# The small loads of a decode kernel in fewer pieces: 32 rows of w4 in one load, the last rows of wo in three loads instead of eight

## The chip, the cores and the metric

The kernel runs on one core of a Trainium2 chip. A core has a matrix engine (PE, with its own stream of weight loads, PEld), a vector engine (DVE), a scalar engine (ACT), a general engine (POOL) and a queue engine (SP) that here does nothing but issue loads and the one store. Sixteen DMA engines move the data from memory. The metric is the device time of one launch in microseconds (us); less is better. All tensors are bfloat16 in memory.

## The reference

One decode step for one token of width 512. The token is normalised; from it come an attention branch over the last 4096 positions of a cache with 32 heads of 128, and a gated MLP branch. The result is `x + attention * silu(mlp)`.

```python
x = A_x                                   # [1, 1, 512]
xn = _layernorm(x, axis=-1)
# attention: 32 heads of 128, the last W = 4096 of 32768 cached positions
q = (xn @ wq).reshape(1, 1, 32, 128).transpose(0, 2, 1, 3)
k, v = k_cache[:, :, Sk - W:, :], v_cache[:, :, Sk - W:, :]
p = softmax(einsum("bhqd,bhkd->bhqk", q, k) * 128 ** -0.5)
s = einsum("bhqk,bhkd->bhqd", p, v).transpose(0, 2, 1, 3).reshape(1, 1, 4096) @ wo   # wo [4096, 512]
# MLP: with one token the shifted parts are zero, so hs = zeros @ w2
x1 = xn + hs
h2 = gelu(_layernorm(x1) @ w3) @ w4       # w3 [512, 1376], w4 [1376, 512]
g = silu(x1 + h2)
return x + s * g
```

Keys and values of the window are 32 MB each; `wq` and `wo` are 4 MB each. In all the profile counts 78.84 MB that are read from memory.

## The kernel before, in words

Everything is loaded through one helper, `load` (L78, L79), which issues on SP's queue and keeps the order in which the program is written. All of these issues therefore carry line 79 in the profile. Two tiny loads of the token go through ACT's queue.

The weights of the MLP come first: `w2`, `w3`, `w4`. The 1376 rows of `w4` are kept in three parts. 1024 rows fill `w4_sb[:, 0:8, :]`, 8 rows on each of the 128 partitions. The last 32 rows, of 1 KB each, stand in the ninth slot, `w4_sb[0:32, 8, :]`; they are fetched by two loads, one of 7 rows and one of 25. The 320 rows in between go to `w4_few`, by two loads of 20 partitions with 8 KB each. (The profile's names leave digits out: `w_sb` is w2, w3 or w4, and `w_few` is `w4_few`.) Then `wq` follows with 4 MB.

The 32 heads are worked on in 8 groups of four, in a loop over `s` from 0 to 9 with an instruction order on PE, DVE and ACT that is written out by hand. In turn `s` the keys of group `s` (4 MB, `load_kv`) are loaded, and the values of group `h = s - 2`. A group's scores are made half on DVE (multiply, L330, and reduce, L332) and half on PE (transposes, L346, copies by ACT, L348, and matmuls, L354). A softmax follows. The values of groups 0 to 6 are multiplied by `v_part` in wide matmuls (L429), those of group 7 in narrow ones (L438). There are three buffers for keys and two for values, so a load waits until its buffer has been read.

The output projection takes `wo` in blocks of heads: 0 to 15, 16 to 23 and 24 to 27 by `load_wo`, and the last four heads by row. For these, `wo_rows` holds 128 rows of 1 KB for each of the heads 28 to 31. In the last turns the values of group 7 are loaded in four pieces (`cuts`: columns 0 to 64, 64 to 96, 96 to 112 and 112 to 128), so that PE can begin on the first of them. Behind them come the loads of `wo_rows`: for each of the four heads one load of its first 72, 88, 104 or 120 rows, and one of the rest. So 12 loads stand on SP's queue at the end. PE then does `v_part` piece by piece, with the block of heads 24 to 27 (`y_block(2)`) between the first two; DVE divides by the softmax's sum (`v_out`, L455), and `y_head` adds the four heads by four matmuls each (`rows_add`, L157). DVE multiplies by the gate (L605) and adds the token (L607), and SP stores the row.

The tile framework gives each load one of eight completion semaphores, in turn.

Of the kernel before, what the change touches and what calls it, by code (L numbers as in the profile page):

```python
# [8 lines left out]
P = 128  # L9
# [9 lines left out]
G = 4  # L19
# [10 lines left out]
def kernel(  # L30
# [18 lines left out]
    _, H, Sk, Dh = A_k_cache.shape  # L49
# [8 lines left out]
    F = B_w3.shape[1]  # L58
# [19 lines left out]
    def load(dst, src):  # L78
        return tc.keep_in_program_order(nc.sync.dma_start(out=dst, in_=src))  # L79
# [9 lines left out]
    load(w3_sb[:], B_w3.rearrange("(p c) n -> p c n", p=P))  # L89
    w4_sb = wts.tile([P, 9, D], BF16, name="w4_sb")  # L90
    load(w4_sb[:, 0:8, :], B_w4[0:8 * P, :].rearrange("(p c) n -> p c n", p=P))
    load(w4_sb[0:7, 8, :], B_w4[F - 32:F - 25, :])
    load(w4_sb[7:32, 8, :], B_w4[F - 25:F, :])
    w4_few = wts.tile([64, 8, D], BF16, name="w4_few")
    nc.gpsimd.memset(w4_few[:], 0.0)
    for c in range(2):
# [7 lines left out]
    def load_kv(pool, cache, g, cuts=(0, CP)):  # L104
        t = pool.tile([P, CP, Dh], BF16, tag="kv", name="kv")
        src = cache[0, G * g:G * g + G, W0:, :].rearrange("a (b c) d -> b a (c d)", b=PB)
        dst = t[:].rearrange("p c d -> p (c d)")
        for c0, c1 in zip(cuts, cuts[1:]):
            load(dst[:, c0 * Dh:c1 * Dh], src[:, :, c0 * Dh:c1 * Dh])
        return t  # L110
# [43 lines left out]
    def rows_add(ps, col, w, last):  # L154
        k = col.shape[0]
        for j in range(KC):
            nc.tensor.matmul(ps[32 * j:32 * j + 1, :], lhsT=col, rhs=w[0:k, j * P:(j + 1) * P],  # L157
                             start=False, stop=last, skip_group_check=True)
# [161 lines left out]
    def k_open(g):  # L320
        st[g] = {
            "sT": ps_s.tile([P, CP - 64, G], FP32, tag="sT", name="sT"),
            "S": sm_pool.tile([P, CP], FP32, tag="S", name="S"),
        }

    def k_vector(g, kn, part):
        m = nd(g) // 4
        rows = slice(m * part, m * part + m)
        prod = prod_pool.tile([P, 20, Dh], BF16, tag="prod", name="prod")
        nc.vector.tensor_tensor(out=prod[:, 0:m, :], in0=kn[:, rows, :],  # L330
                                in1=q_bc[:, g:g + 1, :].to_broadcast([P, m, Dh]), op=ALU.mult)
        nc.vector.tensor_reduce(out=st[g]["S"][:, rows], in_=prod[:, 0:m, :], axis=AX.X, op=ALU.add)  # L332
# [3 lines left out]
    def batches(g):  # L336
        n, m = nd(g), CP - nd(g)
        k = -(-m // 8)
        edges = [n + m * i // k for i in range(k + 1)]
        return list(zip(edges, edges[1:]))  # L340

    def k_turn(g, kn, b):
        c0, c1 = batches(g)[b]
        pt = ps_tr.tile([P, 8, P], BF16, tag="pt", name="pt")
        for c in range(c0, c1):
            nc.tensor.transpose(pt[:, c - c0, :], kn[:, c, :], ident_bf[:])  # L346
        kts[b] = kt_pool.tile([P, 8, P], BF16, tag="kt", name="kt")
        nc.scalar.copy(out=kts[b][:, 0:c1 - c0, :], in_=pt[:, 0:c1 - c0, :])  # L348

    def k_scores(g, b):  # L350
        kt = kts.pop(b)
        c0, c1 = batches(g)[b]
        for c in range(c0, c1):
            nc.tensor.matmul(st[g]["sT"][:, c - nd(g), :], lhsT=kt[:, c - c0, :],  # L354
                             rhs=qT_bf[:, G * g:G * g + G], start=True, stop=True)
# [39 lines left out]
    def sm_den(g):  # L395
        s = st[g]
        s["den"] = ps_misc.tile([P, G], FP32, tag="misc", name="den_ps")
        nc.tensor.matmul(s["den"][:], lhsT=ones_f[:], rhs=s["sum"][:], start=True, stop=True)

    def sm_rden(g):  # L400
        s = st[g]
        s["rden"] = sm_pool.tile([P, G], FP32, tag="rden", name="rden")
        nc.vector.reciprocal(out=s["rden"][:], in_=s["den"][:])  # L403
# [4 lines left out]
    h_part = H - G  # L408
    o_blk, wo_blk, ox_blk = {}, {}, {}

    def load_wo(i):
        h0, n = blocks[i]
        load(wo_blk[i], A_wo[h0 * P:(h0 + n) * P, :].rearrange("(p t) n -> p t n", p=P))
# [1 line left out]
    def wo_row(h):  # L415
        return wo_rows[:, h - h_part, :]

    def load_rows(h, p0, p1):
        load(wo_rows[p0:p1, h - h_part, :], A_wo[h * P + p0:h * P + p1, :])

    def v_part(g, v, c0=0, c1=CP):
        s = st[g]
# [18 lines left out]
    def v_add(g):  # L441
        s = st[g]
        s["oT"] = ps_misc.tile([P, G], FP32, tag="misc", name="oT")
        for j in range(4):
            nc.tensor.matmul(s["oT"][:], lhsT=s["ov_sb"][:, j, :], rhs=fold[:, G * j:G * j + G],  # L445
                             start=(j == 0), stop=(j == 3))

    def v_out(g):
        h = G * g
        b = [i for i, (h0, _) in enumerate(blocks) if h >= h0][-1]  # L450
        if b not in o_blk:
            o_blk[b] = sm_pool.tile([P, blocks[b][1]], BF16, tag=f"o{b}", bufs=1, name="o")
        c = h - blocks[b][0]
        if g >= NG - 3:
            nc.vector.tensor_tensor(out=o_blk[b][:, c:c + G], in0=st[g]["oT"][:], in1=st[g]["rden"][:],  # L455
                                    op=ALU.mult)
            return
        for k in range(G):
            nc.scalar.mul(o_blk[b][:, c + k:c + k + 1], st[g]["oT"][:, k:k + 1], st[g]["rden"][:, k:k + 1])  # L459
# [51 lines left out]
    for s in range(NG + LAG):  # L511
        h = s - LAG
        last = h == NG - 1
        kn = load_kv(k_pool, A_k_cache, s, (0, 64, CP) if s == 0 else (0, CP)) if s < NG else None
        if s == LAG:
            wts_guard.__exit__(None, None, None)
            v_pool = ctx.enter_context(tc.tile_pool(name="v", bufs=V_BUFS))
            wo_blk[2] = v_pool.tile([P, 4, D], BF16, tag="wo_4", bufs=1, name="wo_4")
            wo_rows = v_pool.tile([P, H - h_part, D], BF16, tag="wo_rows", bufs=1, name="wo_rows")
        if last:  # L520
            v = load_kv(v_pool, A_v_cache, h, cuts)
            for r, p in zip(range(H - G, H), (72, 88, 104, 120)):
                load_rows(r, 0, p)
                load_rows(r, p, P)
        elif h >= 0:
            v = load_kv(v_pool, A_v_cache, h)
        if h == 3:
            wo_24 = k_pool.tile([P, 32, D], BF16, tag="kv", name="wo_24")
            wo_blk[0], wo_blk[1] = wo_24[:, 0:16, :], wo_24[:, 16:24, :]
            load_wo(0)  # L530
        if h == 5:
            load_wo(1)
            load_wo(2)

        if s < NG:
            nb = len(batches(s))

            def keys(b0, b1):
                for b in range(b0, b1):
                    k_turn(s, kn, b)  # L540
                    if b > 0:
                        k_scores(s, b - 1)

            k_open(s)
            k_vector(s, kn, 0)
            keys(0, 2)
            if s > 1:
                sm_den(s - 2)
                sm_rden(s - 2)
            if h - 1 in MOVED:  # L550
                v_add(h - 1)
                v_out(h - 1)
            if s == 7:
                rows_add(y_ps, one_f, y_row, False)
            keys(2, 4)
            k_vector(s, kn, 1)
            if s > 0:
                sm_turn(s - 1)
            if s == 6:
                ox_spread(0)  # L560
            keys(4, nb)
            k_scores(s, nb - 1)
            sm_own(s)
            if s > 0:
                sm_exp(s - 1)
            k_vector(s, kn, 2)
            if s == 6:
                ox_pick(0)
            k_vector(s, kn, 3)
            if h >= 0:  # L570
                v_part(h, v)
            sm_max(s)
            if s == 6:
                y_wide(0, 0, 16)
            if h >= 0 and h not in MOVED:
                v_out(h)
        elif s == NG:

            sm_den(NG - 2)
            sm_rden(NG - 2)  # L580
            sm_turn(NG - 1)
            sm_exp(NG - 1)
            v_add(h - 1)
            v_out(h - 1)
            ox_spread(1)
            ox_pick(1)
            sm_den(NG - 1)
            sm_rden(NG - 1)
            y_block(1)
            v_part(h, v)  # L590
            v_add(h)
            v_out(h)
            ox_spread(2)
        else:
            v_part(h, v, 0, cuts[1])
            ox_pick(2)
            y_block(2)
            for c0, c1 in zip(cuts[1:], cuts[2:]):
                v_part(h, v, c0, c1)
            v_out(h)  # L600
            for r in range(H - G, H):
                y_head(r)
# [36 lines left out]
```

## Time and profile before

| what | value |
|---|---|
| median of three runs | 196.84 us (196.53 to 197.04) |
| the profiled execution: time, span | 196.84 us, 195.0 us |
| busy: PE, DVE, ACT | 138.5 us (71%), 145.6 us (75%), 90.6 us (46%) |
| DMA: packets, bytes, mean rate | 4765, 79.08 MB, 405 GB/s |
| mean granted PE clock | 0.666 |

The span runs from the first to the last instruction; 1.84 us of the profiled execution's time lie outside it. Each "slice" of the page is a fortieth of the span, 4.9 us, and its digits are tenths of busy time. In a line of the chain the first number is the start and the second the length, both in us. A DMA's line there runs from its issue to its landing. SPq is SP's issuing queue.

### The profile page before, as it was taken

The numbers are of one execution on the slowest core, as the hardware profiler recorded it, in microseconds if no ns is written. First come the engines' busy times: TensorE is split into PE (matmuls) and PEld (weight loads), VectorE is DVE, ScalarE is ACT, GpSimd is POOL, SyncE is SP. The second block draws the span as 40 slices with busy tenths as digits, with TensorE's granted clock in tenths as the row PEclk, the third lists the DMA queues.
The fourth block names the chain that finished last, engine by engine and source line by source line (L and its number), as shares of the span: only waits on it lengthen the run. The fifth ranks groups of instructions, "written<-read, shape, count | busy, mean of one in ns | idle before, by whom it ended". The sixth has DMA issues, their size and how long they took to land.

```text
span 195.0 us, 3926 instructions
## 1 busy us (share of the span) xinstructions
PE 138.5 (71%) x1696; PEld 100.0 (51%) x1696; DVE 145.6 (75%) x168; ACT 90.6 (46%) x197; POOL 5.9 (3%) x12
## 2 busy tenths in 40 slices
PE   0548978989955169249869892974497989868852
PEld 0447248867855153248438642942483358644640
DVE  1580012999999999998999999999999988932001
ACT  2003002888778265308855752582277157861100
POOL 8210000000000000000000000000000000000000
PEclk9999985555555555855885557588555795885855
DMA  6999999999999999999999999999999999999950
GB/s 207 444 432 417 420 440 444 425 440 430 430 427 439 437 447 430 430 430 430 420 430 440 430 417 403 460 430 430 427 423 432 433 427 399 448 400 405 390 172 4
DMA packets 4765, 79.08 MB, mean 405 GB/s; under 512 B 709, under 2 KB 1253, under 8 KB 1765
## 3 DMA queue, kind: packets, MB, share of 16 engines
q1 hardware_dynamic: 4597, 78.84, 95.4%
q8 instruction: 13, 0.21, 0.4%
q10 hardware_dynamic: 152, 0.00, 0.0%
q14 instruction: 3, 0.02, 0.0%
HBM read 78.84 MB, written 0.00 MB: 404 GB/s over the span
## 4 chain that ended last, share of the span: by engine, by line
DVE 49%; PE 28%; DMA 11%; ACT 4%; issue 4%; SPq 1%; POOL 0%; POOLq 0%; ACTq 0%
DVE S L332 29%; DVE prod L330 15%; DMA kv<-in_A_v_cache_dram 8%; PE pt L346 6%; PE oT L445 4%; ACT kt L348 3%; PE hr_ps L256 3%; PE ov L429 3%; PE a_ps L237 2%; PE sT L354 2%; DMA x_bf<-in_A_x_dram 2%; PE yr_ps L493 2%; PE qT_ps L272 2%; PE hr_ps L251 1%; DVE S L368 1%
## 5 line engine op out<-in xcount | busy, mean ns | idle before, releaser
L332 DVE TENSOR_REDUCE S<-prod 128x20 f32<-128x2560 bf16 (+2 forms) x32 | 82.2, 2570 | 1.1
L348 ACT COPY kt<-pt 128x1024 bf16<-128x1024 bf16 (+1 forms) x56 | 55.2, 1006 | 16.8 <-PE pt L346 15.8
L346 PE MATMUL pt<-ident_bf,kv 128*128 128x128 bf16 x444 | 51.4, 293 | 2.4 <-DMA kv<-in_A_k_cache_dram 2.4
L346 PEld LDWEIGHTS <-kv 128*128 128x128 bf16 x444 | 41.9, 136 | 7.4 <-issue 3.5
L330 DVE TENSOR_TENSOR prod<-kv,q_bc 128x2560 bf16<-128x2560 bf16 (+2 forms) x32 | 43.5, 1359 | 1.7 <-ACT q_bc L286 1.3
L354 PE MATMUL sT<-qT_bf,kt 128*128 128x4 bf16 x444 | 20.9, 169 | 13.3 <-ACT kt L348 12.2
L354 PEld LDWEIGHTS <-kt 128*128 128x128 bf16 x444 | 17.6, 106 | 21.1 <-ACT kt L348 20.7
L429 PE MATMUL ov<-kv,pT 128*16 128x512 bf16 x224 | 22.3, 569 | 0.0
L445 PE MATMUL oT<-fold,ov_sb 128*128 128x4 f32 x56 | 11.5, 328 | 13.7 <-DVE rden L403 12.7
L445 PEld LDWEIGHTS oT<-fold,ov_sb 128*128 128x128 f32 x56 | 10.8, 289 | 14.7 <-DVE rden L403 13.2
L392 ACT ACTIVATE pT<-S,mb 128x128 bf16<-128x128 f32 x32 | 13.9, 576 | 0.3
L429 PEld LDWEIGHTS <-pT 128*16 128x16 bf16 x224 | 6.4, 116 | 12.9 <-issue 11.9
L459 ACT ACTIVATE o<-oT,rden 128x1 bf16<-128x1 f32 x20 | 3.6, 264 | 20.3 <-PE oT L445 20.3
L433 ACT COPY ov_sb<-ov 128x512 f32<-128x512 f32 x7 | 4.1, 590 | 15.3 <-PE ov L429 15.3
L455 DVE TENSOR_TENSOR o<-oT,rden 128x4 bf16<-128x4 f32 x3 | 0.5, 162 | 12.7 <-PE oT L445 8.3
L363 ACT ACTIVATE own<-sT,par 128x48 f32<-128x48 f32 (+2 forms) x32 | 7.6, 361 | 3.7 <-PE sT L354 3.7
L392 ACT ACTIVATION_READ_ACCUMULATOR pT<-S,mb 128x1 f32 x32 | 8.4, 261 | 0.0
L240 ACT ACTIVATE a_bf<-a_ps 128x8 bf16<-128x8 f32 x1 | 0.2, 178 | 14.4 <-PE a_ps L237 14.4
L259 DVE COPY hr<-hr_ps 1x512 f32<-1x512 f32 x1 | 0.7, 678 | 7.5 <-PE hr_ps L256 7.5
L376 PE MATMUL mt_ps<-ident_f,m 128*1 128x128 f32 x8 | 2.9, 360 | 4.4 <-DVE rden L403 4.4
L237 PE MATMUL a_ps<-z_bf,w_sb 128*128 128x1 bf16 (+2 forms) x68 | 4.8, 204 | 1.5 <-DVE z_bf L220 1.5
L237 PEld LDWEIGHTS <-w_sb 128*128 128x128 bf16 (+2 forms) x68 | 5.0, 166 | 1.6 <-issue 1.6
(119 smaller groups left out, 102.1 us busy)
## 6 DMA issues: line engine op xcount, KB each, us to landing
kv<-in_A_k_cache_dram SPq DMA_DIRECT2D x7, 4096.0 KB
kv<-in_A_v_cache_dram SPq DMA_DIRECT2D x7, 4096.0 KB
wq_sb<-in_A_wq_dram SPq DMA_DIRECT2D x1, 4096.0 KB
kv<-in_A_k_cache_dram SPq DMA_DIRECT2D x2, 2048.0 KB
wo<-in_A_wo_dram SPq DMA_DIRECT2D x1, 2048.0 KB
kv<-in_A_v_cache_dram SPq DMA_DIRECT2D x1, 2048.0 KB
w_sb<-in_B_w_dram SPq DMA_DIRECT2D x1, 1376.0 KB
w_sb<-in_B_w_dram SPq DMA_DIRECT2D x1, 1024.0 KB
```

What stands on the lines that cost most here:

```text
L237: nc.tensor.matmul(a_ps[0:m, j:j + 1], lhsT=w3_cols(c, j), rhs=z3_bf[:, c:c + 1], start=(c == 0), stop=(c == KC - 1))
L256: nc.tensor.matmul(hr_ps[:], lhsT=act, rhs=w, start=False, stop=(i == len(chunks) - 1))
L330: nc.vector.tensor_tensor(out=prod[:, 0:m, :], in0=kn[:, rows, :], in1=q_bc[:, g:g + 1, :].to_broadcast([P, m, Dh]), op=ALU.mult)
L332: nc.vector.tensor_reduce(out=st[g]["S"][:, rows], in_=prod[:, 0:m, :], axis=AX.X, op=ALU.add)
L346: nc.tensor.transpose(pt[:, c - c0, :], kn[:, c, :], ident_bf[:])
L348: nc.scalar.copy(out=kts[b][:, 0:c1 - c0, :], in_=pt[:, 0:c1 - c0, :])
L354: nc.tensor.matmul(st[g]["sT"][:, c - nd(g), :], lhsT=kt[:, c - c0, :], rhs=qT_bf[:, G * g:G * g + G], start=True, stop=True)
L363: nc.scalar.mul(s["own"][:, 0:m, a], s["sT"][:, 0:m, a], par[:, a:a + 1])
L392: nc.scalar.activation(out=s["pT"][:, :, a], in_=s["S"][:], func=ACT.Exp, scale=scale, bias=mb[:, a:a + 1], accum_out=s["sum"][:, a:a + 1])
L429: nc.tensor.matmul(s["ov"][r:r + 4 * G], lhsT=s["pT"][:, c:c + 4, :].rearrange("p i a -> p (i a)"), rhs=v[:, c:c + 4, :], start=False, sto ...
L433: nc.scalar.copy(out=s["ov_sb"][:], in_=s["ov"][:])
L445: nc.tensor.matmul(s["oT"][:], lhsT=s["ov_sb"][:, j, :], rhs=fold[:, G * j:G * j + G], start=(j == 0), stop=(j == 3))
```

## The change

The two loads for the last 32 rows of `w4` become one load. The eight loads for the last rows of `wo` become three: one for heads 28 and 29 together, one for head 30 and one for head 31, each over all 128 partitions. What is loaded, where it is put in the on-chip memory, and all computation stay as they were.

```diff
     load(w4_sb[:, 0:8, :], B_w4[0:8 * P, :].rearrange("(p c) n -> p c n", p=P))
-    load(w4_sb[0:7, 8, :], B_w4[F - 32:F - 25, :])
-    load(w4_sb[7:32, 8, :], B_w4[F - 25:F, :])
+    load(w4_sb[0:32, 8, :], B_w4[F - 32:F, :])
...
-    def load_rows(h, p0, p1):
-        load(wo_rows[p0:p1, h - h_part, :], A_wo[h * P + p0:h * P + p1, :])
+    def load_rows(h, n):
+        load(wo_rows[:, h - h_part:h - h_part + n, :],
+             A_wo[h * P:(h + n) * P, :].rearrange("(h p) n -> p h n", p=P))
...
             v = load_kv(v_pool, A_v_cache, h, cuts)
-            for r, p in zip(range(H - G, H), (72, 88, 104, 120)):
-                load_rows(r, 0, p)
-                load_rows(r, p, P)
+            for r, n in ((H - G, 2), (H - 2, 1), (H - 1, 1)):
+                load_rows(r, n)
```

## The prediction

> **What bounds the kernel now.** I read the slices of the page first, for what is busy when. The DMA row is full from the second slice to the 38th, while no compute engine is:
>
> ```profile
> span 195.0 us, 3926 instructions
> ...
> DMA  6999999999999999999999999999999999999950
> GB/s 207 444 432 417 420 440 444 425 440 430 430 427 439 437 447 430 430 430 430 420 430 440 430 417 403 460 430 430 427 423 432 433 427 399 448 400 405 390 172 4
> ```
>
> So the time is the loads plus what comes after the last of them. The chain that ended last, from 173 us on, says which load that is (columns: start, length, what):
>
> ```profile
> 173.67 15.92 DMA kv<-in_A_v_cache_dram
> ...
> 189.60 1.70 DMA wo_rows<-in_A_wo_dram
> ...
> 191.34 0.30 PE y_ps L157 x4
> ...
> 191.66 0.30 DVE y L605
> ...
> 191.99 0.29 DVE out_row L607
> ```
>
> The last piece of the last values lands at 189.58, and only then is the last `wo_rows` load *issued*; it lands 1.70 us later, four matmuls follow, and the store. The waits of SP's queue from 172 us on say why it was issued so late (total, times, longest):
>
> ```profile
> SPq L79 <- DMA kv<-in_A_v_cache_dram: 12.6, 5, 4.7
> ```
>
> The loads take eight completion semaphores in turn: the numbers that the trace records at their issues repeat with period eight. A load is therefore held until the one eight places before it has landed. Five of the eight `wo_rows` loads are held by values: they go out at 178.37, 183.33, 186.00, 187.39 and 189.60, each 0.01 to 0.02 us after the landing of group 6's values (178.35) and of the four pieces (183.31, 185.99, 187.37, 189.58).
>
> The third view is the trace's landing marks: each load leaves 16, one from each DMA engine that it uses and the rest at its issue. The `wq` load's come in groups: ten at 19.76 to 20.27, one at 21.54, five at 22.41 to 22.57. Those five stay behind: for group 6's values the first mark is at 174.40, the last at 178.35, and most of the final 4 us of trailing is that old. A whole 4 MB load adds 9.7 us to every engine, whether ahead or behind, and the values of the last group are issued (171.79) before the most advanced engine runs dry (174.40). So no engine ever waits, and the kernel ends when the most trailing engine has worked off its own list.
>
> Fourth, the last stretch by windows (window, its length, busy time of PE, PEld, DVE, ACT and POOL, clock, DMA share, GB/s):
>
> ```profile
> 178.00:183.50 5.50, 4.80 (x72) 2.27 (x65) 0.11 (x1) 0.59 (x1) 0.00 (x0) 0.73 0.98 410
> 184.50:186.00 1.50, 1.02 (x40) 0.93 (x41) 0.35 (x2) 0.00 (x0) 0.00 (x0) 0.50 0.86 270
> 186.00:188.60 2.60, 2.01 (x64) 1.68 (x64) 0.00 (x0) 0.00 (x0) 0.00 (x0) 0.50 0.65 199
> ```
>
> From 184.5 the engines are still 86% busy, but move a third less: while the first engines work at row pieces of 1 KB packets, a 4 KB packet of values takes 0.18 to 0.22 us instead of 0.16. This stretches the last pieces on the trailing engine. On the foremost engine the second, third and fourth piece take 2.47, 1.27 and 1.25 us; on the last one 2.68, 1.38 and 2.21, together 1.28 us more.
>
> **The profiled execution** took 196.84 us, its span 195.0 and 1.84 around it; that is also the median of the three times. All sums start there.
>
> **The w4 rows.** Two loads, of 7 and of 25 rows of 1 KB, become one of 32. The 7-row load leaves seven marks and the 25-row load five: one row on each of seven engines, then five on each of five. A load with 128 rows leaves 16; I take 16 for 32 rows as well, two rows each. A 1 KB packet took 0.046 us there, so an engine that served both pieces falls from 6 x 0.046 = 0.28 to 2 x 0.046 = 0.09: 0.18 us less. One that served neither gains 0.09. The next load, `w_few`, also leaves five marks, and moves 64 KB on each of five engines, eight packets of 8 KB at 0.31 = 2.5 us, which is just how far five engines trail afterwards. If the two fives are the same, the trailing engine gains 0.18; if not, it loses up to 0.09. I take -0.18, and keep +0.09 for the range. Since it is never idle, this reaches the end.
>
> [...]
>
> **SP's queue.** One issue fewer at the start and five fewer at the end, at 0.27 to 0.56 us each; the issues for 128 rows that remain take about 0.55 each. At the start the turns move by one place (the second half of K group 0 and K groups 1 and 2 go out behind other loads), with the engines fed until 22 us by what is already out: nothing. At the end the three row loads take turns whose holders landed by 168.63, so they go out from about 174.3 to 176, right behind the values. Behind them on SP's queue is only the output store. No wait is added on any compute engine: the merged load of heads 28 and 29 is the first of the three and its 16 rows pass before those of head 30.
>
> **The tail after the last values.** Before: 189.58 to the end of the last matmul at 191.64, 2.06 us. Afterwards two things can end last there.
>
> ```profile
> 185.94 0.59 PE L157 MATMUL y_ps<-wo,ox 128*1 128x128 bf16 x16 [0.48 <-DMA wo_rows<-in_A_wo_dram]
> ...
> 190.25 0.16 DVE L455 TENSOR_TENSOR o<-oT,rden 128x4 bf16<-128x4 f32 x1 [4.36 <-PE oT L438]
> 190.47 0.10 PEld L157 LDWEIGHTS <-o 128*1 128x1 bf16 x8 [0.34 <-DVE o L455]
> ```
>
> PE: the last values, their scaling and the start of the output rows take 190.47 - 189.58 = 0.89, and 16 such matmuls that wait for nothing 0.59 (the first line): 1.48. The rows: on the trailing engine 32 rows follow the values. In this trace the 24-row load, with which 32 rows have passed there, landed at 190.92, 1.34 after the values. Add 0.04 to release PE and 0.30 for the last four matmuls: 1.68. The larger counts: 2.06 becomes about 1.65 (three completion marks instead of six), **-0.41**. Ends: -0.58 (PE alone) and -0.05 (rows at 0.052 us each, as at 188.5 to 189: 32 x 0.052 + 0.34 = 2.0).
>
> **The stretch of the last pieces.** The change keeps 512 rows of 1 KB, but every engine now takes its 32 directly behind its values. So foremost engines are done by about 185.3 instead of coming back for more at 184.6, 187.2 and 188.65, and others take more rows than they did. The nearest rows differ: packets of 8 KB beside the 25-row load at 9.5 us were not stretched at all (0.309), those beside rows at 184.5 by a third. Ends: -1.28 (no stretch at all) and +0.4 (512 rows against the some 380 that were moved before the last values had landed, 1.28 x 132/380). I take **-0.2**: the row traffic stays, but the late pieces beside the trailing engine's last five packets (0.24 to 0.35 us each from 187.5 to 188.66) go, for about 0.3, against more rows before.
>
> [...]
>
> Sum: 196.84 - 0.18 - 0.41 - 0.20 = **196.05 us**. With the next stages (L605, L607, the store) as they were.
>
> **Rivals.**
> *The stretch goes altogether* (the pieces cause it): 196.84 - 0.18 - 0.41 - 1.28 = 195.0. For it: before 184 eleven engines read 4 KB packets at 0.16. Against: the rows remain.
> *The stretch grows*, as all rows are now out early: 196.84 - 0.18 - 0.41 + 0.4 = 196.65, no change. For it: packets of values stretched as soon as rows moved.
> *Slower: an instruction fetch on the trailing engine.* The trace has 13 fetches of 16 KB, each on one engine; the one at 33.99 put an engine that was foremost 1.54 us behind the others. Those before 187 fell on engines that were not last. The fetch order may move with the instructions left out. If one falls on the trailing engine: 196.05 + 1.54 = 197.6, or 197.8 with the stretch as before. It decides from some 1.4 us on. Against: PE's stream loses only a few waits, and the fetch at 187.21 comes when the trailing engine has only a few packets left.
> *The change does nothing*: were the row loads held by turns as before, only -0.18 is left: 196.65.
>
> **How the numbers follow.** What a measurement of this kernel can tell from no change is 0.3%, 0.59 us: 196.25 to 197.43 is "same". Forecast case 0.47, its own range 195.6 to 196.45; stretch gone 0.20; stretch grown, or nothing done, 0.23; slower 0.10. Faster: three quarters of the first and all of the second, with a little of the third, 0.60. Same: 0.31. Slower: 0.09. The range 195.1 to 196.9 leaves out a part of the second case and the slower one.
>
> **What would show it.** Right: no waits of SP's queue for values after 176; all three `wo_rows` issues before 176.5; the last four of the 16 output matmuls less than 1.7 us after the last values' landing; the 32-row load with 16 marks; five trailing engines behind by 0.2 less at `wq`. Wrong: a wait for `wo_rows` of over 0.6 us at the end; last values landing after 189.6; a landing spread of group 6's values over 4 us.

## The result, and the profile after

The changed kernel took 195.19 us (median of 6 runs, 195.06 to 195.96), the kernel before 196.98 beside it; the ratio is 0.9914 (95% interval 0.9893 to 0.9936), about 1.7 us less. In six later runs its median was 195.58 and the ratio 0.9928 (0.9901 to 0.9955). The profiled execution took 195.15 us, with 1.75 outside its span.

From the page:

```profile
span 193.4 us, 3919 instructions
...
DMA  6999999999999999999999999999999999999970
GB/s 209 426 444 417 427 427 441 425 434 430 434 430 429 434 430 434 434 434 427 424 434 434 430 434 400 458 434 434 430 427 427 425 420 392 462 420 410 396 298 5
```

The row of busy shares differs from before in the second last slice alone (7 instead of 5), and the rate of that slice is higher (298 against 172 GB/s). The chain that ended last (start, length, what):

```profile
173.74 14.60 DMA kv<-in_A_v_cache_dram
...
188.39 0.60 PE oT L440 x16
...
189.02 0.17 DVE o L457
...
189.23 0.73 PE y_ps L156 x16
```

No `wo_rows` load stands in it any more. The last values land at 188.34 (before 189.58), and the last output matmul ends at 189.96 (before 191.64). So of the 1.68 us, 1.24 were gained ahead of that landing and 0.44 behind it. The chain puts all 16 output matmuls down to PE; the trace's single records show a short wait in them. Twelve have started by 189.41, the last `wo_rows` load lands at 189.61, and the last four start at 189.66. SP's issues, and the waits of its queue from 172 us on:

```profile
171.86 2.49 SPq L79 DMA_DIRECT2D kv<-in_A_v_cache_dram  x4
174.39 1.61 SPq L79 DMA_DIRECT2D wo_rows<-in_A_wo_dram  x3
190.63 0.61 SPq L79 DMA_DIRECT2D out_dram<-out_row  x1
```

```profile
SPq L79 <- DVE out_row L608: 12.1, 1, 12.1
...
SPq L79 <- DMA kv<-in_A_v_cache_dram: 2.4, 1, 2.4
```

The row loads go out directly behind the values. One wait for values is left, from 176.0 to 178.44: what stands next in the queue then is the output store, which has nothing to store for another 12 us. By windows (length, busy PE, PEld, DVE, ACT, POOL, clock, DMA share, GB/s):

```profile
178.00:183.50 5.50, 4.80 (x71) 2.27 (x64) 0.18 (x1) 0.58 (x1) 0.00 (x0) 0.72 0.98 409
184.50:186.00 1.50, 1.08 (x41) 0.98 (x37) 0.35 (x2) 0.00 (x0) 0.00 (x0) 0.52 0.99 382
186.00:188.60 2.60, 2.18 (x72) 1.88 (x72) 0.01 (x1) 0.00 (x0) 0.00 (x0) 0.50 0.58 209
```

From 184.5 to 186 the engines move 382 GB/s at a share of 0.99, where before it was 270 at 0.86. By the landing marks, the second, third and fourth piece of the values take 2.46, 1.26 and 1.24 us on the last engine, together 4.96 instead of 6.27.

On the marks: in both traces a load of 128 partitions has 16 of them, and so has the one of 32 rows here. The smaller loads of weights have a single record at their issue and then fewer marks: 7 for the 7 rows of `w4`, 5 for the 25 and for each load of `w4_few`, and 12, 14, 11, 10, 13, 12, 15 and 8 for the `wo_rows` loads of 72, 56, 88, 40, 104, 24, 120 and 8 rows. That each mark is one engine's, with an equal share of the load, is the author's reading; no trace names the engine.

### The profile page after: what moved, and what is told of

Read it like the earlier page. It is cut to its first block, busy times and chain, and to the rows that moved or that the text cites. A ratio compares the mean times of both kernels' runs of the same rounds, so it can differ in the third digit from the quotient of the medians.

```text
span 193.4 us, 3919 instructions
## 1 busy us (share of the span) xinstructions
PE 138.4 (72%) x1696; PEld 100.3 (52%) x1696; DVE 145.6 (75%) x168; ACT 90.6 (47%) x197; POOL 5.9 (3%) x12
## 4 chain that ended last, share of the span: by engine, by line
DVE 50%; PE 29%; DMA 10%; ACT 4%; issue 4%; SPq 1%; POOL 0%; POOLq 0%; ACTq 0%
DVE S L331 29%; DVE prod L329 15%; DMA kv<-in_A_v_cache_dram 8%; PE pt L345 6%; PE oT L447 4%; ACT kt L347 3%; PE hr_ps L255 3%; PE ov L431 3%; PE a_ps L236 2%; PE sT L353 2%; DMA x_bf<-in_A_x_dram 2%; PE yr_ps L495 2%; PE qT_ps L271 2%; PE hr_ps L250 1%; DVE S L367 1%
```

## The experiments

Two explanations were to be told apart for the 1.24 us. **A**: the rows in loads of fewer than 128 partitions slow all that moves beside them, and whole loads do not. **B**: the row loads were late because their turns held them. Ratios are to the kernel before on the same chip. Unless its diff says otherwise, a kernel is the changed one. "The rows" are those of `wo_rows`.

**One part of the change alone.** Rows as changed, `w4` as before:

```diff
-    load(w4_sb[0:32, 8, :], B_w4[F - 32:F, :])
+    load(w4_sb[0:7, 8, :], B_w4[F - 32:F - 25, :])
+    load(w4_sb[7:32, 8, :], B_w4[F - 25:F, :])
```

> The change without its part on w4: the 32 rows stay in two loads of 7 and 25 rows, the last rows of wo go in three whole loads. Theory (the w4 part is worth nothing at the end, because which engine trails is set by more than those rows): the same time as the changed kernel, within 0.15 us, so about 1.7 us under the kernel before; pieces of the last values unstretched, 2.5, 1.27 and 1.27 us on the last engine. Rival (the w4 part is worth the 0.18 us that was forecast): 0.18 us slower than the changed kernel, and the last landing mark of group 6's values later by that.

Measured: 195.86 us median of 12 (195.05 to 197.13), ratio 0.9948 (0.9921 to 0.9975). The fastest run equals that of the changed kernel, but 8 of 12 lie above 195.6. In its profile (196.34 us) the pieces are as quick as in the changed kernel (2.52, 1.27, 1.26) and the last values land at 188.43. Its chain ends on PE instead:

```profile
188.52 1.81 PE oT L441 x64
...
190.57 0.62 PE y_ps L157 x12
```

PE's matmuls on the values run until 190.33, 1.9 us after they have landed, so this run says nothing against the rows' gain. It shows that PE is now close behind the DMAs; the last two experiments go into that. The expectation was missed by the median all the same: it lies 0.6 us above that of the changed kernel's 12 runs below (195.26), where 4 of 12 are above 195.6.

The other part alone, the kernel before with `w4` in one load:

```diff
-    load(w4_sb[0:7, 8, :], B_w4[F - 32:F - 25, :])
-    load(w4_sb[7:32, 8, :], B_w4[F - 25:F, :])
+    load(w4_sb[0:32, 8, :], B_w4[F - 32:F, :])
```

> Only the part on w4: one load of 32 rows, the last rows of wo in the eight pieces of before. Theory: no change that can be told, ratio 0.998 to 1.002, the last pieces stretched as before (2.7, 1.4 and 2.2 us on the last engine) and the last row load issued after the last values. Rival (w4 worth 0.18 us): ratio 0.999; both cannot be told apart by the time alone, but by the landing marks after w4_few: five engines behind the others by 0.2 us less than before.

Measured: 196.77 us (196.66 to 197.45), ratio 0.9996 (0.9986 to 1.0006). Nothing. The pieces are stretched as before (2.71, 1.42 and 2.24 us), and the end of the chain is that of before:

```profile
189.64 1.68 DMA wo_rows<-in_A_wo_dram
...
191.36 0.31 PE y_ps L156 x4
```

Alone, the part on `w4` gives nothing, and the rows alone give 1.0 us by the median (196.83 to 195.86). Whether one load for `w4` adds something beside them, or the first of these kernels had more of the long runs by chance, is not settled.

**Divided, but early.** Four loads of 72 and 56 partitions; for heads 28 to 30 together, then for 31:

```diff
-            for r, n in ((H - G, 2), (H - 2, 1), (H - 1, 1)):
-                load_rows(r, n)
+            for r, n in ((H - G, 3), (H - 1, 1)):
+                load_rows(r, n, 0, 72)
+                load_rows(r, n, 72, P)
```

> The changed kernel with the last rows in four loads of 72 and 56 rows (heads 28 to 30 together, then head 31, each 0:72 and 72:128). Four loads are too few to be held by values, so none is issued late, but their rows don't fall on the engines as a 128-partition load does. Theory A (the division of the rows stretches the values' packets): 4 KB packets at 0.18 to 0.22 us again from 184 on, the last values 0.6 to 1.3 us later than in the changed kernel, and 40 instead of 32 rows behind them on twelve engines, 0.3 us: 196.0 to 196.8 us. Theory B (what stretched them was the late issue, with rows arriving while the queues run empty): packets at 0.16, last values at 188.3, 195.2 to 195.6 us.

Measured: 196.67 us (196.41 to 197.18), ratio 0.9994 (0.9983 to 1.0005): no gain. Three of the four loads go out by 174.05, and yet:

```profile
184.50:186.00 1.50, 1.02 (x34) 0.70 (x31) 0.35 (x2) 0.00 (x0) 0.00 (x0) 0.50 0.96 252
186.00:188.60 2.60, 1.66 (x52) 1.43 (x48) 0.00 (x0) 0.00 (x0) 0.00 (x0) 0.50 0.76 216
```

The engines are 96% busy and move 252 GB/s. A 4 KB packet of values takes 0.22 us in the mean once rows move, and the last values land at 189.52. Early issue is not what the gain came from.

**Whole, but held.** Eight loads of all 128 partitions and half the columns, so that the turns hold them as before:

```diff
+            for r in range(H - G, H):
+                load_rows(r, 0, D // 2)
+                load_rows(r, D // 2, D)
```

> The changed kernel with the last rows in eight loads, each of all 128 partitions and half of the columns of one head (512-byte packets instead of 1 KB). Eight loads are held by the values as before, the last one until the last values have landed. Theory A (the division stretches, the holding delays only the tail): values unstretched, last values at 188.3; the last row load goes out then and lands 1.7 us later, tail 2.06 instead of 1.64: about 195.6 us. Theory B (the late issue stretches): last values at 189 to 189.6 and 196.3 to 197 us.

Measured: 195.81 us (195.5 to 196.8), ratio 0.9953 (0.9936 to 0.9969). The pieces run unstretched (2.51, 1.23, 1.25), and the last values land at 188.04, as in the changed kernel. What is lost is the tail:

```profile
186.81 3.15 DMA wo_rows<-in_A_wo_dram
...
190.00 0.46 PE y_ps L156 x3
```

The last matmul ends at 190.46, 2.42 us after the last values (1.62 in the changed kernel). So A is the 1.24 us, and B is only the tail.

**Even, with all engines.** Halves of 64 partitions, in loads that leave 16 marks, so four partitions to a mark, early:

```diff
+            for r, n in ((H - G, 3), (H - 1, 1)):
+                load_rows(r, n, 0, 64)
+                load_rows(r, n, 64, P)
```

> The changed kernel with the last rows in four loads of 64 rows (heads 28 to 30 together, then head 31, each 0:64 and 64:128), none issued late. [...] It parts two readings of what stretches the packets of values. By partitions (an engine that writes where other engines write): stretched again, 4 KB packets at 0.18 us and more from 184 on, last values at 189 or later, 196.2 to 196.8 us. By the number of engines (fewer than 16): unstretched at 0.16, last values at 188.3, 195.1 to 195.5 us.

Measured: 197.13 us (196.97 to 198.51), ratio 1.0019 (1.0002 to 1.0036): the worst of all. Each load leaves 16 marks, as a whole one does, but:

```profile
184.50:186.00 1.50, 1.02 (x41) 0.93 (x42) 0.35 (x2) 0.00 (x0) 0.00 (x0) 0.60 0.97 239
186.00:188.60 2.60, 1.59 (x56) 1.22 (x46) 0.00 (x0) 0.00 (x0) 0.00 (x0) 0.50 0.86 208
```

4 KB packets take 0.24 us in the mean beside the rows, and 1 KB packets 0.067 instead of 0.046. The last values land at 190.41. With the marks read as engines, uneven shares or too few engines are thereby out as the whole cause. What still differs is which partitions a load covers, or which engine writes them; no run here shows the latter.

**120 and 8 partitions.** As above with 120 in place of 64: a load of 120 partitions leaves 15 marks, so 8 partitions to a mark, as many as in a load of 128 with its 16; the 8 partitions leave eight marks.

```diff
+            for r, n in ((H - G, 3), (H - 1, 1)):
+                load_rows(r, n, 0, 120)
+                load_rows(r, n, 120, P)
```

> The rows as four early loads: partitions 0 to 120 of heads 28 to 30, partitions 120 to 128 of them, and the same two for head 31. A load of 120 partitions takes 15 DMA engines with 8 partitions each, as many for each engine as in a load of 128. Theory 1 (an engine slows the others where it writes partitions that are another engine's in the loads of values, and in those an engine has 8 neighbouring partitions): the 120-row loads are in step with the values for all but the last engine, so 4 KB packets stay at 0.16 us, the last values land at 188.2 to 188.8 and the time is 195.1 to 195.8. Theory 2 (the same, but an engine's partitions in a load of 128 are not neighbours): 4 KB packets at 0.20 to 0.33 us from 184, the last values at 189.4 to 190.4 and the time 196.5 to 197.1. Rival (any load of less than 128 partitions slows the others): as theory 2.

Measured: 196.59 us (196.24 to 197.35), ratio 0.999 (0.9968 to 1.0012). The forecast of theory 1 is missed: 4 KB packets take 0.22 to 0.26 from 186.5 to 188, and 1 KB packets 0.064 to 0.092 until 189.25. Its mechanism is not refuted by this. The first 66 rows, from 185.57 to 186.5, all belong to loads of 120 partitions; they took 0.046 us each, and the 4 KB packets beside them 0.16 from 185.75 to 186.25. The stretch sets in at 186.5, and the foremost engine, at some 0.0425 us from row to row, is through with its 24 rows at about 186.6 and comes to a load of 8 partitions. With 72 partitions the stretch came after 0.5 us of rows, well before the foremost engine had left its first load (18 rows). And two things are mixed in this profile: from 183.25 to 185.5, when no row had moved yet, the 4 KB packets were at 0.17 to 0.22 already, while those of 8 KB kept their 0.31; that is the second stretch, below. Whether the 120 partitions, the 8, or any division stretches the packets stays open.

Packets in the last stage of the profiles, in us:

| rows in loads of | 4 KB, from the first row on | 1 KB row | last values land | median time |
|---|---|---|---|---|
| before: 72 to 120 and the rest | 0.189 | 0.055 | 189.58 | 196.98 |
| 72 / 56 | 0.219 | 0.057 | 189.52 | 196.67 |
| 64 / 64 | 0.241 | 0.067 | 190.41 | 197.13 |
| 120 / 8 | 0.197 | 0.067 | 189.31 | 196.59 |
| 128, half columns | 0.161 | (0.5 KB: 0.028) | 188.04 | 195.81 |
| 128: the change | 0.162 | 0.046 | 188.34 | 195.19 |

**Is the start to be mended too?** In the changed kernel five engines trail at `wq` (five marks at 22.29 to 22.66 us, ten at 19.87 to 20.43), and the two loads of `w4_few` leave five marks each. Here there are five loads of eight partitions, every fourth one, to bring in eight engines, as the 8-row load of the kernel before has eight marks (the lines for the two old loads, the view `w4_mid` and the matching change of the mask `few` are left out):

```diff
...
+    for j in range(4):
+        load(w4_few[j:32:4], w4_mid[j:j + 1].rearrange("j e n -> e (j n)"))
+    load(w4_few[32:64:4], B_w4[8 * P + 256:8 * P + 320, :].rearrange("(e t) n -> e (t n)", e=8))
```

> The changed kernel with the 320 rows of w4_few in five loads of 8 partitions, spread over eight engines (40 KB each) instead of two loads over five engines (64 KB each). It takes 24 KB, 0.93 us, off the five engines that trail. Theory (the most trailing DMA engine sets the landing of the last values, PE's own order follows close behind): last values at about 187.4 instead of 188.34, but the output matmuls bound by PE's chain, which has some 0.4 us to give: 194.8 us. Rival (which engine trails is not set by w4_few): 195.2 us as before, last values at 188.3. Rival (DMA alone bounds the end): 194.3 us.

Measured: 196.09 us (195.69 to 197.99), ratio 0.9962 (0.9934 to 0.9989): slower than the changed kernel by 0.9, where 0.4 less was forecast. The last values land at 189.15 instead of the forecast 187.4. The spread of `wq`'s marks falls as expected, from 2.79 to 1.78 us, but all marks are late: the first is at 21.49 instead of 19.87. From 9 to 13 us, first this kernel, then the changed one:

```profile
9.00:13.00 4.00, 1.24 (x5) 1.15 (x6) 3.20 (x22) 0.00 (x0) 0.55 (x1) 1.00 1.19 401
```

```profile
9.00:13.00 4.00, 1.24 (x5) 1.16 (x6) 3.20 (x22) 0.00 (x0) 0.55 (x1) 1.00 1.09 459
```

Eight 32 KB packets of `wq` beside these loads took 2.46 to 2.94 us instead of 1.21, while the loads' own 8 KB packets kept 0.31. That this is the same stretch is not shown. And not every load of fewer than 128 partitions stretches its neighbours: in the kernels before and after, the two loads of `w4_few`, of 20 partitions and five marks, stand beside the same packets of `wq`, and from 10.5 to 13 us these took 1.21 to 1.25.

The same kernel with two of PE's blocks of output rows moved behind the values, `y_block(1)` behind `v_part` of group 6 and `y_block(2)` behind the third piece:

```diff
-            y_block(1)
             v_part(h, v)
+            y_block(1)
...
-            y_block(2)
             for c0, c1 in zip(cuts[1:], cuts[2:]):
+                if c1 == CP:
+                    y_block(2)
                 v_part(h, v, c0, c1)
```

> As the one before, and two blocks of PE's work moved: the matmuls of heads 16 to 23 behind group 6's values (into the wait for ACT's copy), those of heads 24 to 27 behind the third piece of the last values. PE gains about 1 us before the last values. Theory: now the landing of the last values bounds again: 187.4 + 1.64, 194.2 us. Rival (PE was not the bound): the same time as without the move.

Measured: 196.08 us (195.69 to 197.76), ratio 0.9963 (0.994 to 0.9985): no difference from the order here.

**PE's order.** The same move of the two blocks (the last diff) in the changed kernel, with `w4_few` as it was:

> The changed kernel with only those two blocks of PE's work moved. Theory (DMA bounds the changed kernel in most executions, PE where its clock falls earlier): median 195.1, hardly lower than the changed kernel, but with less spread upwards (195.0 to 195.4). Rival (PE bounds it): 194.7 us.

Measured: 195.05 us (194.91 to 195.8), ratio 0.9901 (0.9885 to 0.9918). Once more, with the changed kernel beside it:

> The changed kernel once more, beside the next one. Expected: a ratio of 0.990 to 0.994 to the kernel before, fastest runs at 195.0 to 195.1; the median 195.2 where PE's clock falls to half late, up to 0.7 more where it falls before the values of group 6.

> The changed kernel with the two blocks of output rows moved behind the values (y_block(1) behind v_part(6), y_block(2) behind the third piece), once more. Theory (PE's chain of values is close behind the DMAs and sets the end in the runs in which its clock falls early; the order gives it room): median 0.1 to 0.4 us under the changed kernel's and fewer runs above 195.6. Rival (the order does nothing): medians within 0.1 us.

Measured: 195.58 (194.99 to 196.14), ratio 0.9928 (0.9901 to 0.9955), and 195.05 (194.99 to 195.97), ratio 0.9912 (0.9887 to 0.9937). Over all 12 runs of each the medians are 195.26 and 195.05, with 4 and 2 runs above 195.6. The order may be worth 0.2 us; the intervals overlap.

Both profiled executions here were long ones (195.77 and 195.97), and so show what makes them. PE between 170 and 172 us in the first profile of the changed kernel, and in its second one (the third value from the right is the granted clock, 1.00 and 0.50):

```profile
170.00:172.00 2.00, 1.82 (x32) 0.62 (x31) 1.81 (x3) 1.95 (x12) 0.00 (x0) 1.00 1.04 442
```

```profile
170.00:172.00 2.00, 2.00 (x17) 0.54 (x20) 1.66 (x3) 1.95 (x11) 0.00 (x0) 0.50 1.08 459
```

In that second profile, at the clock of 0.50, the matmuls of group 5's values end at 173.43 instead of 171.85. The last values wait for their buffer, so their loads go out later:

```profile
173.48 3.00 SPq L79 DMA_DIRECT2D kv<-in_A_v_cache_dram  x4
176.52 2.00 SPq L79 DMA_DIRECT2D wo_rows<-in_A_wo_dram  x3
```

The foremost engine is done with group 6's values at 174.37 by its mark. The first 16 KB packet of the last values starts at 174.81 (173.74 in the first profile) and takes 1.31 us (0.90 there, 0.61 mostly), and the first mark of the first piece comes at 181.12 instead of 179.52. And from 183.5 to 186 the 4 KB packets take 0.20 to 0.26 us, before any row moves, while 8 KB packets stay at 0.31. The last values land at 188.94, and PE, whose clock was 0.54 from 178 to 183.5 us, is behind them too: its matmuls on them run until 189.64.

**The buffer.** As the kernel with the moved blocks, with the last values in the buffer of the keys of group 6, which is free long before:

```diff
+        if s == NG - 2:
+            k6 = kn
...
-            v = load_kv(v_pool, A_v_cache, h, cuts)
+            v = load_kv(v_pool, A_v_cache, h, cuts, k6)
```

> As the kernel with the moved blocks, but the last values go into the buffer of the keys of group 6, which is free early, instead of the one that the values of group 5 leave: their loads no longer wait for PE's multiplication of group 5's values, which ended at 171.85 in the changed kernel's profile and at 173.4 to 173.5 where PE's clock had fallen to half before it. Theory (in the later runs the loads go out after 172.9, the foremost DMA engines run dry, and the 4 KB packets of values then take 0.19 to 0.26 us with no row under way): the four issues of the last values come before 171, whatever PE's clock, 4 KB packets stay at 0.16, the last values land at 188.0 to 188.5, median 194.9 to 195.1 and at most one run above 195.6. Rival (what ends late in those runs is PE's own chain, and the DMAs don't matter): median 195.0 to 195.3, and the runs above 195.6 stay, as 2 of 12 before.

Measured: 194.96 us (194.85 to 195.03, 4 runs), ratio 0.9909 (0.9892 to 0.9925). All issues of values are done by 156.1. In the profile PE takes 3.25 us for group 5's values instead of 1.90, near the 3.07 of the long run at clock 0.50, and it costs nothing:

```profile
155.51 32.50 DMA kv<-in_A_v_cache_dram
...
188.06 0.60 PE oT L441 x16
...
188.90 0.75 PE y_ps L157 x16
```

4 KB packets are at 0.161 throughout, and the last values land at 188.01. It is the fastest kernel here. Its median is 0.3 below the changed kernel's over 12 runs, with intervals that overlap. That none of its four runs is long is what the theory says, but four are too few to prove it (at 2 in 12 none of four is long about half the time), and PE also began group 5's values 1.3 us earlier than in the long run of the changed kernel. How much of a long run is the late loads and how much PE's own chain is not settled.

## Why the prediction was right, and where not

The forecast was 196.05 us with 195.1 to 196.9 as the range; the time is 195.19. The direction is right, and the value lies at the range's lower end, since one term was taken some six times too small. What happened is the first rival: "the stretch goes altogether", at 195.0. That the time is inside the range at all, by 0.1 us, is luck: two terms were off in opposite directions, and with the 0.18 forecast for `w4` it would have been outside.

**The tail** was right, in size and in what sets it: -0.41 was said, and -0.44 measured (2.06 to 1.62). The prediction held the rows for the longer of two ways to the end (1.68 us, PE alone 1.48), and so it is: the last row load lands 1.27 us after the values (1.34 said), the last four matmuls start 0.05 later and end 0.30 after that. Without this wait they would have started at about 189.51 instead of 189.66, by the spacing of the 16 that wait for nothing. The held loads with whole partitions confirm it from the other side: there the tail is 2.42. One step on the way there was an estimate: that 32 rows had passed the trailing engine at 190.92 is rows divided by marks, added up over six loads (6 + 4 + 8 + 4 + 8 + 2). For the first four this makes 22, while the 0.83 us from 189.58 to the last mark of the 40-row load at 190.41 are 18 rows at 0.046.

**SP's queue** was right in its issues: 174.39, 175.03 and 175.55, all before 176.5. "No waits for values after 176" was not met to the letter: the store's wait until 178.44 was overlooked, and costs nothing.

**The w4 rows** were wrong: -0.18 was taken, and alone they brought nothing (ratio 0.9996; what they do beside the whole rows is open, see above). That the five engines of the 25-row load are the five of `w4_few`, on which the term rests, no run shows. The load does leave 16 marks, and the five engines do trail by less at `wq` in the mean (2.38 instead of 2.53 us behind the ten). But the last of them was at 22.66 instead of 22.57, and the spread of group 6's values was 4.20 us, above the 4 us that the prediction had named as a sign against itself. The trailing engine is one of five, picked by their scatter at `wq` (0.16 us before, 0.37 here) and by the short instruction fetches of 8 KB, which by the marks set the engine that serves them back by 0.65 to 0.95 us and hit one or two of the five; a mean over five is not the last of them.

**The stretch of the last pieces** is the step that failed. Taken was -0.2; the three pieces gave -1.31 (6.27 to 4.96), beside +0.07 at the landing of the first. Even the part that was granted was too small: in the record the trailing engine's last four packets (not five) took 0.24 to 0.35 us, together 0.48 over 0.16 each, where 0.3 was taken. The end -1.28 was in the text and was argued down: "the row traffic stays". It stays, 512 packets in both profiles, and does no harm in loads of 128 partitions: 0.162 us for a 4 KB packet beside rows at 0.046. In the kernel before, all 31 packets of 4 KB that start from 184.6 to 185.1 took 0.18 to 0.22 us. That they stretched alike is no sign against the pieces as the cause: with 72/56 and 64/64 too, every 4 KB packet that starts from 184.5 to 185 takes 0.23 us or more, and the 64/64 halves, which by their 16 marks share the work most evenly, suffer most (0.241 us in the mean).

That the division causes the stretch is shown, by the runs with whole and divided loads: 4 KB packets take 0.161 and 0.162 us beside rows in whole loads, 0.219 and 0.241 beside 72/56 and 64/64, and from 184.5 to 186 us the engines move 382 GB/s beside the change's whole loads, 252 and 239 beside these. By what mechanism it does is not shown; the run with 120 and 8 partitions (0.22 to 0.26 us from 186.5 to 188) does not settle it, and which engine writes which partitions no run here shows.

**The slower rival**, a fetch on the trailing engine, did not occur in the profile: the fetches of 16 KB cost an engine some 1.55 us each again by the marks, but none hit the trailing one.

## What to carry to other kernels

Where loads move beside a stream of 128-partition loads, try them at 128 partitions first: the same bytes in pieces of 64 to 120 partitions and their rests made the 4 KB packets beside them 17 to 49% longer at the end of this kernel (0.189 to 0.241 us instead of 0.162), and loads of eight strided partitions stood beside doubled packets at its start (2.46 to 2.94 us instead of 1.21). It is no law: two loads of 20 partitions cost the packets of `wq` nothing (1.21 to 1.25). So look at the packets. Read the packet times and the GB/s beside the share of busy DMA engines: 97% busy at 239 GB/s (64/64) is not a full pipe, with 382 at 99% in the same window of the changed kernel. When a bound is taken away, look at what is close behind it; in the profiled long runs here that was PE at a clock of 0.50, which also set a buffer free late (at 173.43 us instead of 171.85 in one).

## What the hardware showed that was not expected

- Some divided loads stretch the others' packets: 4 KB from 0.16 to 0.22 (72/56) and 0.24 us (64/64) in the mean. Others don't: beside the two loads of `w4_few`, of 20 partitions, packets of 32 KB stayed at 1.21 to 1.25. What decides is open.
- Beside five loads of eight strided partitions, eight packets of 32 KB took 2.46 to 2.94 us instead of 1.21; the reason is open.
- A second stretch needs no rows: where the last values were issued at 173.2 to 173.6 (in the second profile of the changed kernel the foremost engine is done at 174.37 and the first packet of the last values starts at 174.81), 4 KB packets took 0.17 to 0.26 us in means over half a microsecond while 8 KB packets kept 0.31. With the issues at 152.77 to 156.1 it was not there. Its mechanism is open.
- PE's granted clock falls to half at different moments from run to run: at 170 to 172 us it was 1.00 in one profile of the changed kernel and 0.50 in another, and the same 32 matmuls took 1.90 and 3.07 us.
